# One K block and its V block held together through a pass of a four-pass attention kernel, and summed there as p k v^T

## The chip, the core and the metric

The kernel runs on one core of a Trainium2 chip. The metric is device time in microseconds (us) of one execution, compared as medians over several runs.

## The reference, cut to what matters

One decode step through attention, dense, attention, dense (each with a layer norm and a residual), and the gradients of everything with respect to the input, both caches and all weights. Both attention layers use the same caches and the same weights: 32 query heads, 4 key/value groups of 8 heads, 65,536 cached positions, head size 128, bfloat16. K and V are 64 MiB each.

```python
def _A_ref(x, k_cache, v_cache, wq, wo):
    q = (x @ wq).reshape(B, Sq, Hq, Dh).transpose(0, 2, 1, 3)
    k = jnp.repeat(k_cache, rep, axis=1)
    v = jnp.repeat(v_cache, rep, axis=1)
    scores = jnp.einsum("bhqd,bhkd->bhqk", q, k) * (Dh ** -0.5)
    p = _softmax(scores, axis=-1)
    o = jnp.einsum("bhqk,bhkd->bhqd", p, v)
    return o.transpose(0, 2, 1, 3).reshape(B, Sq, Hq * Dh) @ wo
...
x = x + _A_ref(_layernorm(x), A_k_cache, A_v_cache, A_wq, A_wo)
x = x + _B_ref(_layernorm(x), B_w1, B_b1, B_w2, B_b2)
x = x + _A_ref(_layernorm(x), A_k_cache, A_v_cache, A_wq, A_wo)
x = x + _B_ref(_layernorm(x), B_w1, B_b1, B_w2, B_b2)
...
_out, _vjp = jax.vjp(_f, A_x, A_k_cache, A_v_cache, A_wq, A_wo, ...)
```

The gradient with respect to q of one head, written for one position c with weight p_c, is dq = sum over c of p_c (v_c . dO - delta) k_c, where delta is a number for the head. It can be split: (sum p_c k_c v_c^T) dO - delta (sum p_c k_c). The two sums need K, V and p, but not dO.

## The kernel before, in words

**Four passes over the caches.** Pass 1 (`attn_fwd(0, ...)`, called at line 1643) is the forward of the first attention, pass 2 (`attn_fwd(1, ...)`, line 1683) that of the second, pass 3 (`attn_bwd3`, lines 1207 to 1295) gives dq of the second attention, pass 4 (`attn_bwd4`, lines 1298 to 1486) gives dq of the first and the gradients of both caches. Between the passes stand dense stages: 1 to 2, 2 to 3 and 3 to 4.

**Blocks and buffers.** A cache is cut into 4 groups of 16 blocks; a block is 32 columns of 128 positions, 1 MiB, written here as V(3,12): group 3, block 12. SBUF holds an arena of 20 buffers of one block each (line 267). Eight of them become "planes" with the exponentials of one layer and group (`plane`, line 276); a plane is held from when its group starts (`holds`, lines 1183 to 1185) until pass 4 is done with it. The other buffers carry K, V, weights and staged outputs. `Slot`, `take_one` and `take_pair` (lines 284 to 333) give a buffer, or two neighbours for a 2 MiB load, in the order in which they became free when the program is written. A load into a buffer waits on the chip until the buffer's last reader is done. All these loads are issued by one queue (SP), in order: a load whose buffer is not free holds up those behind it.

**The order of the work.** A pass goes through 8-column items, 256 of them. `pipeline` (line 847) runs one step per item: in pass 2 the transposes of K (`kT`, line 1023), two steps later the scores (`kS`, line 1037), 36 steps later P times V (`v8`, line 1121), and at the end of the step one piece of background work (`bg.step`, line 869), as small products with wq or wo. In passes 1 to 3 the order on TensorE, VectorE and ScalarE inside the pipeline is the written one (`manual_schedule`); in pass 4 a scheduler decides. `kv8` (line 351) loads a block when it is first touched, `kv_done` (line 377) frees it after its last item.

**Blocks kept between passes.** Each pass goes through the blocks in an order of its own (`ITEMS`, line 411). `plan_keep` (line 416) keeps 8 K blocks from pass 1 to pass 2, and 7 V blocks each from pass 2 to 3 and from 3 to 4: those that the next pass touches first. K kept from pass 1 and V kept from pass 3 are kept transposed, in place (`turned_to`, line 369); the next pass then needs no transposes for them. Pass 2 begins with K(3,12); pass 3 comes to block (3,12) in its last quarter group; pass 4 begins with the V blocks (3,15) down to (3,9), so V(3,12) is one of the 7 that pass 3 keeps.

**PSUM.** In passes 1 to 3 the pool has three banks for transposes (`ps_tr`), two for scores, one accumulator, one for the background and one for small things (`ps_mv`, line 100): the two tiny transposes of each softmax unit, among others.

The lines that the change touches:

```python
            if i is None:
                sl = Slot("blk_" + t, load=True)
                nc.sync.dma_start(out=sl.t.rearrange("p (j d) -> p j d", d=DH), in_=half(KVIN[t], g, hb))
```

Of the kernel before, what the change touches and what calls it, by code (L numbers as in the profile page):

```python
# [16 lines left out]
P = 128  # L17
# [3 lines left out]
def kernel(  # L21
# [57 lines left out]
    slotp = ctx.enter_context(tc.tile_pool(name="slotp", bufs=1))  # L79


    PS = {}

    def open_psum(stack, name, pass4=False):
        PS["pool"] = stack.enter_context(tc.tile_pool(name=name, bufs=1, space=PSUM))
# [12 lines left out]
        return PS["pool"].tile(shape, F32, name="ps_acc", tag="acc", bufs=1)  # L98

    def ps_mv(shape, dtype=F32):  # L100
        if PS["pass4"]:
            return ps_tr(shape, dtype)
        return PS["pool"].tile(shape, dtype, name="ps_mv", tag="mv", bufs=1)

    def ps_bg(shape):
        return PS["pool"].tile(shape, F32, name="ps_bg", tag="bg", bufs=1)
# [244 lines left out]
    def kv8(t, g, c8):  # L351
        hb, j = divmod(c8, J)
        key = (t, g, hb)
        have = KV["have"]
        if key not in have:
            i = None
            if NOW["pairs"] and hb % 2 == 0 and (t, g, hb + 1) not in have and key not in KV["halves"]:
                i = take_pair()
            if i is None:
                sl = Slot("blk_" + t, load=True)  # L360
                nc.sync.dma_start(out=sl.t.rearrange("p (j d) -> p j d", d=DH), in_=half(KVIN[t], g, hb))
                have[key] = sl
            else:
                for h in range(2):
                    have[(t, g, hb + h)] = Slot("blk_" + t, at=i + h)
                nc.sync.dma_start(out=wide(i).rearrange("p (j d) -> p j d", d=DH), in_=KVIN[t][g][hb // 2])
        return have[key].t.rearrange("p (j d) -> p j d", d=DH)[:, j:j + 8, :]

    def turned_to(t, g, c8, kb8):

        if KV["turn"] == t and (t, g, c8 // J) in KV["keep"]:
            state_key = (t, g, c8)
            KV["next"].add(state_key)
            return kb8
        return ktpool.tile([P, 8, P], BF, name="kt", tag="kt")

    def kv_done(t, g, c8):

        key = (t, g, c8 // J)
        if c8 % J == J - 8 and key not in KV["keep"]:  # L380
            KV["have"].pop(key).free()

    def order_by_unit(desc, unit):
# [25 lines left out]
    DV_LAG = TLEAD + 1  # L409
    V_LEAD = 4 * J // 8  # L410
    ITEMS = [order_by_unit(False, SU), order_by_unit(True, SU), order_by_unit(False, HB), order_by_unit(True, J)]
    V_SHIFT = lambda k: min(V_LEAD, max(0, (k - V_LEAD) // 3))
    TOUCH = [touch_order(ITEMS[0], [("k", 0), ("v", FWD_LAG)]), touch_order(ITEMS[1], [("k", 0), ("v", FWD_LAG)]),
             touch_order(ITEMS[2], [("v", 0), ("k", B3_LAG)]), touch_order(ITEMS[3], [("v", V_SHIFT), ("k", B4_LAG + V_LEAD)])]
# [6 lines left out]
    def start_pass(p):  # L421
        KV["keep"] = plan_keep(p)
        KV["turned"] = KV.get("next", set())
        KV["next"] = set()
        KV["turn"] = {0: "k", 2: "v"}.get(p)
        NOW["pairs"] = p < 3
        KV["halves"] = set(TOUCH[p][-8:] + (TOUCH[p][:18] if p else []))

    def f_cols(ap, nb):
        return ap[:, bass.ds(512 * (nb // 4) + nb % 4, P, step=4)]  # L430
# [353 lines left out]
    class Background:  # L784
# [8 lines left out]
        def step(self, i):  # L793
            while self.later and i >= self.later[0][0]:
                self.add(*self.later.popleft()[1:])
            while self.urgent:
                r = next(self.urgent[0][1], "end")
                if r == "end":
                    self.urgent.popleft()
                    continue  # L800
                if r == "wait":
                    break
                return
            while self.normal and self.done < self.total * i / self.steps:
                if next(self.normal[0], "end") == "end":
                    self.normal.popleft()
                else:
                    self.done += 1
                    return

        def add(self, gen, key=None):
            self.urgent.append((key, gen))
# [31 lines left out]
        for fn in TASKS.pop(i, ()):  # L844
            fn()

    def pipeline(items, stages, bg, end=(), holds=(), lead=None):

        def due(lag):
            at = {}  # L850
            for k, it in enumerate(items):
                at.setdefault(k + lag + LEAD if lead is None or lag >= 0 else k + ~lag + lead(k), []).append(it)
            return at
        LEAD = 0 if lead is None else lead(len(items))
        when = [due(l) for _, l in stages]
        maxlag = max(l for _, l in stages) + LEAD
        for i in range(len(items) + maxlag):
            NOW["i"] = i
            NOW["wide"] = NOW["pairs"]
            for at, k in holds:  # L860
                if i == at:
                    hold(k)
            tasks(i - 0.5)
            for n, (fn, lag) in enumerate(stages):
                for it in when[n].get(i, ()):
                    fn(*it)
                if n == 0:
                    tasks(i)
            bg.step(max(0, i - LEAD))
            NOW["wide"] = False  # L870
            NOW["step"] += 1
            for before, fn in end:
                if i == len(items) + maxlag - before:
                    fn()
        while TASKS:
            k = min(TASKS)
            NOW["i"] = int(k + 0.5)
            tasks(k)
# [128 lines left out]
    def attn_fwd(p, L, on_group, bg, end=()):  # L1007
# [113 lines left out]
        def v8(g, c8):  # L1121
# [7 lines left out]
            for i in range(8):  # L1129
# [2 lines left out]
                NOW["ps_o"] = nc.tensor.matmul(ps_o[:, 0:w, :], lhsT=vb8[:, i, :], rhs=E(p, g, c, w),  # L1132
                                               start=(c % SU == 0), stop=(c % SU == SU - 1), skip_group_check=True)
            kv_done("v", g, c8)
            if (c8 + 8) % SU == 0:
                first_at(1, lambda: unit_end(g, su, ps_o))

        def unit_sums(g, su):

# [43 lines left out]
        holds = [(k * n + 2, plane(p, g)) for k, g in enumerate(order) if k > 0]  # L1183
        if p == 0:
            holds.append((len(items) - 40, plane(1, ITEMS[1][0][0])))
        with tc.manual_schedule(engines=ORDERED):
            pipeline(items, [(kT, 0), (kS, TLEAD), (v8, FWD_LAG)], bg, end, holds)
        st.close()


# [16 lines left out]
    def attn_bwd3(p, L, on_group, bg, end=()):  # L1207
# [5 lines left out]
        state = {}  # L1213
        gfirst = {g: next(c8 for gg, c8 in items if gg == g) for g in range(G)}
        glast = {g: [c8 for gg, c8 in items if gg == g][-1] for g in range(G)}

        def vT(g, c8):
            bg.need(g)
# [12 lines left out]
        def vS(g, c8):  # L1231
# [5 lines left out]
            vt = state.pop(("vt", g, c8))  # L1237
            for i in range(8):
                s = (c8 + i) % HB
                if s == 0:  # L1240
                    state["ps_dp"] = ps_sc([P, HB, R])
                late = c8 + i - s == gfirst[g]
                w = min(8, HB - s)

                def delta(first):
                    nc.tensor.matmul(state["ps_dp"][:, :, :].rearrange("p c r -> p (c r)"), lhsT=sel2[:, :],
                                     rhs=state["ndt"][:, :, :].rearrange("o c r -> o (c r)"), start=first, stop=not first,
                                     skip_group_check=True)
                if s == 0 and not late:
                    delta(True)  # L1250
                nc.tensor.matmul(state["ps_dp"][:, s:s + w, :].rearrange("p a b -> p (a b)"), lhsT=vt[:, i, :],
                                 rhs=dOpad[:, g, 0:w, :].rearrange("p a b -> p (a b)"), start=late and s == 0,
                                 stop=(s == HB - 1) and not late, skip_group_check=True)
                if s == HB - 1 and late:
                    delta(False)
            if is_turned("v", g, c8):
                kv_done("v", g, c8)
            if (c8 + 8) % HB == 0:
                c0 = c8 + 8 - HB
                ps_dp = state["ps_dp"]  # L1260

                def ds():
# [6 lines left out]
        def k8(g, c8):  # L1269
            kb8 = kv8("k", g, c8)  # L1270
            dsT = state[("ds", g, c8 // HB)]
            if c8 % SU == 0:
                state["ps_dq"] = ps_acc([P, 8, R])
            ps_dq = state["ps_dq"]
            for i in range(8):
                c = c8 + i
                s = c % HB
                w = min(8, HB - s)
                nc.tensor.matmul(ps_dq[:, 0:w, :].rearrange("p a b -> p (a b)"), lhsT=kb8[:, i, :],
                                 rhs=dsT[:, s:s + w, :].rearrange("p a b -> p (a b)"),  # L1280
                                 start=(c % SU == 0), stop=(c % SU == SU - 1), skip_group_check=True)
            kv_done("k", g, c8)
            if (c8 + 8) % SU == 0:
                su = c8 // SU

                def fold():
                    fold_dq(L, g, su, ps_dq[:, 0, :], gfirst[g] // SU == su, glast[g] // SU == su, dspool)
                    if glast[g] // SU == su:
                        on_group(g)
                first_at(1, fold)  # L1290
# [294 lines left out]

    def open_dense(name):
        st = ExitStack()
        DENSE["pool"] = st.enter_context(tc.tile_pool(name=name, bufs=1))
        return st

# [89 lines left out]
    def on2(g):  # L1680
        if g != lastg[1]:
            bg.add(g_wo(L3, x3, g))
    attn_fwd(1, L3, on2, bg, [(3, pre_load("wo3", lambda: wo_slabs(lastg[1], 2)))])
    bg.drain()

# [29 lines left out]
    def ch_turn(s, js=range(4), to=None):  # L1715

        n = ch_pe(s)
        for j in js:
            pt = ps_tr()
            for kc in range(n):  # L1720
                nc.tensor.transpose(pt[:, kc, :], ch_cols(s, kc, j), ident_b[:, :])
            wt = DENSE["pool"].tile([P, 8, P], BF, name="wt", tag="wt", bufs=8)
            (nc.vector.tensor_copy if (to[j] if to else j == 3) else nc.scalar.copy)(out=wt[:, 0:n, :], in_=pt[:, 0:n, :])
            w1t[(s, j)] = wt

# [132 lines left out]
            bg.add(g_dn(L3, dn3, g, g == firstg[2]))  # L1858
    attn_bwd3(2, L3, on3, bg, [(10, pre_load("wq3", lambda: wq_slabs(lastg[2], 2)))])
    bg.drain()  # L1860


    reset_load()
# [202 lines left out]
```

## Time and profile before

| what | value |
|---|---|
| three runs, us | 1934.89, 1932.82, 1929.56 (median 1932.82) |
| the profiled execution, its own time | 1938.19 us |
| its span, first to last instruction | 1936.3 us |
| mean granted TensorE clock | 0.918 |
| busy: TensorE, VectorE, ScalarE, GpSimd | 82%, 61%, 54%, 7% |
| moved by DMA | 787.62 MB, mean 407 GB/s |

By stage, from the profile's stretches (DMA share is the mean busy share of the 16 DMA engines; it can come out a little above 1):

| stretch, us | stage | TensorE busy | DMA share | GB/s |
|---|---|---|---|---|
| 0 to 365 | pass 1 | 282.31 | 1.00 | 419 |
| 365 to 415 | dense 1 to 2 | 37.69 | 1.01 | 413 |
| 415 to 741 | pass 2 | 263.17 | 1.00 | 419 |
| 741 to 781 | dense 2 to 3 | 37.43 | 0.94 | 320 |
| 781 to 1117 | pass 3 | 271.89 | 1.00 | 418 |
| 1117 to 1172 | dense 3 to 4 | 46.14 | 0.86 | 322 |
| 1172 to 1900 | pass 4 | 622.96 | 1.00 | 408 |
| 1900 to 1936 | last outputs | 22.12 | 0.64 | 262 |

How to read it: a stage with a DMA share of 1 goes as fast as its bytes come; where the share falls, something else ends last. In the timeline rows below, a row is the start, the duration, the engine, the line and the operation; "SPq" is the queue that issues the loads, and a gap between its rows is time in which the next load waited for its buffer.

### The profile page before, as it was taken

The numbers are of one execution on the slowest core, as the hardware profiler recorded it, in microseconds if no ns is written. First come the engines' busy times: TensorE is split into PE (matmuls) and PEld (weight loads), VectorE is DVE, ScalarE is ACT, GpSimd is POOL, SyncE is SP. The second block draws the span as 40 slices with busy tenths as digits, with TensorE's granted clock in tenths as the row PEclk, the third lists the DMA queues.
The fourth block names the chain that finished last, engine by engine and source line by source line (L and its number), as shares of the span: only waits on it lengthen the run. The fifth ranks groups of instructions, "written<-read, shape, count | busy, mean of one in ns | idle before, by whom it ended". The sixth has DMA issues, their size and how long they took to land. (4 is left out here: it accounts for less than half of the span.)

```text
span 1936.3 us, 66770 instructions
## 1 busy us (share of the span) xinstructions
PE 1583.7 (82%) x30099; PEld 1294.0 (67%) x30099; DVE 1172.8 (61%) x2447; ACT 1045.2 (54%) x1620; POOL 143.6 (7%) x325
## 2 busy tenths in 40 slices
PE   6878778588778878978787888778889889688896
PEld 6878777578778878877677776445555556455563
DVE  5645555255555654545454577767867678667685
ACT  3434334245343545436363465757867677567675
POOL 0000000000000000000000002111211111111111
PEclk9989999789998999999999998988988889888896
DMA  9999999999999999999999997999999999999997
GB/s 394 427 427 424 428 429 415 404 421 395 429 425 427 427 419 335 395 426 428 426 420 425 405 363 283 425 422 381 424 424 423 420 399 407 409 415 396 405 421 301
DMA packets 107148, 787.62 MB, mean 407 GB/s; under 512 B 9440, under 2 KB 16622, under 8 KB 42222
## 3 DMA queue, kind: packets, MB, share of 16 engines
q1 hardware_dynamic: 78558, 609.26, 76.2%
q0 software_dynamic: 24080, 165.70, 20.6%
q10 hardware_dynamic: 4224, 8.39, 1.1%
q8 instruction: 235, 3.85, 0.7%
q14 instruction: 51, 0.42, 0.1%
HBM read 617.62 MB, written 165.69 MB: 405 GB/s over the span
## 5 line engine op out<-in xcount | busy, mean ns | idle before, releaser
L164 DVE COPY kt<-ps_tr 128x1024 bf16<-128x1024 bf16 (+1 forms) x733 | 503.3, 688 | 435.7 <-PE ps_tr L1031 237.9
L161 ACT CAST arena<-ps_gg 128x1024 bf16<-128x1024 f32 x457 | 444.4, 1012 | 201.9 <-PE ps_gg L1435 132.0
L1031 PE MATMUL ps_tr<-ident_b,arena 128*128 128x128 bf16 x3840 | 309.1, 225 | 49.3 <-DMA arena<-in_A_k_cache_dram 35.6
L161 ACT COPY kt<-ps_tr 128x1024 bf16<-128x1024 bf16 (+1 forms) x179 | 187.4, 1053 | 185.8 <-PE ps_tr L1225 103.1
L164 DVE CAST arena<-ps_gg 128x1024 bf16<-128x1024 f32 (+2 forms) x186 | 222.3, 1195 | 82.4 <-PE ps_gg L1435 44.4
L1031 PEld LDWEIGHTS <-arena 128*128 128x128 bf16 x3840 | 232.6, 101 | 58.4 <-DMA arena<-in_A_k_cache_dram 38.1
L1132 PE MATMUL ps_acc<-arena 128*128 128x64 bf16 (+4 forms) x4096 | 203.1, 195 | 50.5 <-DMA arena<-in_A_v_cache_dram 32.4
L1435 PE MATMUL ps_gg<-GG,xt 64*128 64x512 bf16 x1024 | 214.3, 414 | 22.0 <-ACT arena L161 10.6
L1354 PE MATMUL ps_tr<-ident_b,arena 128*128 128x128 bf16 x1824 | 179.5, 234 | 38.1 <-DVE kt L164 18.6
L1049 PE MATMUL ps_sc<-L_qpad,kt 128*128 128x64 bf16 (+7 forms) x3584 | 183.1, 194 | 20.8 <-issue 11.0
L1114 ACT ACTIVATE arena<-S_sb,L_negm 128x128 bf16<-128x128 f32 x256 | 165.2, 1006 | 59.4 <-DVE L_negm L1099 51.9
L1132 PEld LDWEIGHTS <-arena 128*128 128x128 bf16 x4096 | 158.2, 100 | 56.6 <-DMA arena<-in_A_v_cache_dram 36.6
L1225 PE MATMUL ps_tr<-ident_b,arena 128*128 128x128 bf16 x2000 | 159.3, 224 | 43.9 <-DMA arena<-in_A_v_cache_dram 42.0
L1354 PEld LDWEIGHTS <-arena 128*128 128x128 bf16 x1824 | 118.9, 104 | 94.2 <-issue 72.8
L1049 PEld LDWEIGHTS <-kt 128*128 128x128 bf16 x3584 | 152.3, 100 | 25.1 <-issue 12.2
L1225 PEld LDWEIGHTS <-arena 128*128 128x128 bf16 x2000 | 120.6, 100 | 49.5 <-DMA arena<-in_A_v_cache_dram 44.7
L1466 PEld LDWEIGHTS <-arena 128*128 128x128 bf16 x2048 | 90.8, 101 | 59.8 <-issue 29.9
L1114 ACT ACTIVATION_READ_ACCUMULATOR arena<-S_sb,L_negm 128x1 f32 x256 | 128.2, 501 | 0.0
L1391 PE MATMUL ps_sc<-DOB,kt 128*128 128x64 bf16 (+3 forms) x1824 | 117.6, 197 | 0.1
L1391 PEld LDWEIGHTS <-kt 128*128 128x128 bf16 x1824 | 84.6, 101 | 48.7 <-issue 47.2
L585 ACT ACTIVATE mv_t<-mv_t 128x1024 bf16<-128x1024 bf16 x96 | 102.0, 1064 | 24.2 <-DVE mv_t L596 24.1
L1466 PE MATMUL ps_acc<-X,arena 128*128 128x64 bf16 (+3 forms) x1536 | 94.7, 197 | 23.5 <-DMA arena<-in_A_k_cache_dram 23.5
(320 smaller groups left out, 2106.0 us busy)
## 6 DMA issues: line engine op xcount, KB each, us to landing
arena<-in_A_k_cache_dram SPq DMA_DIRECT2D x82, 2048.0 KB, 20.7
arena<-in_A_v_cache_dram SPq DMA_DIRECT2D x79, 2048.0 KB, 21.0
out_dram<-arena POOLq DMA_DIRECT2D x149, 1024.0 KB, 15.6
arena<-in_A_v_cache_dram SPq DMA_DIRECT2D x84, 1024.0 KB, 12.5
arena<-in_A_k_cache_dram SPq DMA_DIRECT2D x84, 1024.0 KB, 12.9
arena<-in_A_wo_dram SPq DMA_DIRECT2D x22, 1024.0 KB, 14.9
arena<-in_B_w_dram SPq DMA_DIRECT2D x21, 1024.0 KB, 10.4
arena<-in_A_wq_dram SPq DMA_DIRECT2D x7, 2048.0 KB, 26.2
```

The source lines that it names most:

```text
L161: nc.scalar.copy(out=out, in_=in_)
L164: nc.vector.tensor_copy(out=out, in_=in_)
L585: nc.scalar.activation(out=t[:, :], in_=t[:, :], func=ACTF.Copy, accum_out=y[:, kc:kc + 1])
L1031: nc.tensor.transpose(pt[:, i, :], kb8[:, i, :], ident_b[:, :])
L1049: nc.tensor.matmul(state["ps_s"][:, s:s + w, :].rearrange("p a b -> p (a b)"), lhsT=kt[:, i, :], rhs=L["qpad"][:, g, 0:w, :].rearrange("p ...
L1114: nc.scalar.activation(out=E(p, g, c0, SU)[:, :, h], in_=S[:, h, :], func=ACTF.Exp, bias=L["negm"][:, g, su, h:h + 1], scale=SCALE, accum_ ...
L1132: NOW["ps_o"] = nc.tensor.matmul(ps_o[:, 0:w, :], lhsT=vb8[:, i, :], rhs=E(p, g, c, w), start=(c % SU == 0), stop=(c % SU == SU - 1), skip ...
L1225: nc.tensor.transpose(pt[:, i, :], vb8[:, i, :], ident_b[:, :])
L1354: nc.tensor.transpose(pt[:, i, :], vb8[:, i, :], ident_b[:, :])
L1391: nc.tensor.matmul(state["ps_dp"][:, s:s + w, :].rearrange("p a b -> p (a b)"), lhsT=vt[:, i, :], rhs=DOB[:, g, 0:w, :].rearrange("p a b - ...
L1435: nc.tensor.matmul(pg[:, 512 * h:512 * h + 512], lhsT=xt[64 * h:64 * h + 64, j1 // 8 + m, :], rhs=gg[64 * h:64 * h + 64, :, :].rearrange(" ...
L1466: nc.tensor.matmul(ps_dq[:, 0:w, :].rearrange("p a b -> p (a b)"), lhsT=kb8[:, i, :], rhs=X[:, s:s + w, :].rearrange("p a b -> p (a b)"), ...
```

## The change

Block (3,12), the first that pass 2 touches, is taken out of pass 3 (`ITEMS[2]`). For it pass 2 sums p k v^T for each of the 8 heads of the group (`PKV["m"]`, 128 x 8 x 128, fp32) and p k (`PKV["s"]`), and pass 3 turns these into the block's part of dq by a few small products (`pkv_dq`), added where the unit's dq is folded.

- K(3,12) is still kept from pass 1, but no longer transposed in place: pass 2 transposes it.
- V(3,12) goes into the buffer beside K(3,12) (`i ^ 1`), which is that of K(3,13), and both stay until the sums are made.
- `g_pkv` is a side job of pass 2: one piece per step in which the background did nothing. A piece multiplies 128 x 128 of K by p of four heads on GpSimd (a 128 x 512 product, 64 in all) and multiplies V by an earlier one on TensorE into a PSUM bank, two pieces behind. Four times it adds eight small products for p k.
- That bank is the one of `ps_mv`, so in pass 2 the small things take `ps_tr` banks.
- The dense stage 2 to 3 takes half of its `wt` buffers from the `kt` pool, to make room for `PKV`.
- The plan of what pass 3 keeps for pass 4 (`plan_keep`) is untouched.

```diff
     def ps_mv(shape, dtype=F32):
-        if PS["pass4"]:
+        if PS["pass4"] or PS["m"]:
             return ps_tr(shape, dtype)
...
+    def ps_m():
+        return PS["pool"].tile([P, 4, P], F32, name="ps_m", tag="mv", bufs=1)
...
             if i is None:
-                sl = Slot("blk_" + t, load=True)
+                at = None
+                if key in KV["long"]:
+                    at = have[("k", MG, MB)].i ^ 1
+                    del FREE[at]
+                sl = Slot("blk_" + t, at=at, load=True)
...
-        if KV["turn"] == t and (t, g, c8 // J) in KV["keep"]:
+        if KV["turn"] == t and (t, g, c8 // J) in KV["keep"] and (t, g, c8 // J) != MKEYS[0]:
...
-        if c8 % J == J - 8 and key not in KV["keep"]:
+        if c8 % J == J - 8 and key not in KV["keep"] and key not in KV["long"]:
             KV["have"].pop(key).free()
...
+    MG, MB = ITEMS[1][0][0], ITEMS[1][0][1] // J
+    ITEMS[2] = [(g, c8) for g, c8 in ITEMS[2] if (g, c8 // J) != (MG, MB)]
+    MKEYS = [(t, MG, MB) for t in "kv"]
...
-            bg.step(max(0, i - LEAD))
+            if not bg.step(max(0, i - LEAD)) and sides:
+                if next(sides[0], "end") == "end":
+                    sides.popleft()
...
+        def g_pkv(g, hb):
+            ks, vs = (KV["have"][(t, g, hb)] for t in "kv")
+            k3, v3 = (sl.t.rearrange("p (j d) -> p j d", d=DH) for sl in (ks, vs))
+            nc.vector.memset(PKV["s"][:], 0.0)
+            for hf in range(2):
+                acc = ps_m()
+                made = deque()
+                def product():
+                    j, r = made.popleft()
+                    nc.tensor.matmul(acc[:, :, :].rearrange("p a b -> p (a b)"), lhsT=v3[:, j, :],
+                                     rhs=r[:, :, :].rearrange("p a b -> p (a b)"), start=j == 0, stop=j == J - 1)
+                for j in range(J):
+                    r = spool.tile([P, 4, P], BF, name="pk", tag="pk", bufs=3)
+                    e4 = E(p, g, hb * J + j, 1)[:, 0, 4 * hf:4 * hf + 4]
+                    nc.gpsimd.tensor_tensor(out=r[:, :, :], in0=k3[:, j, :].unsqueeze(1).to_broadcast([P, 4, P]),
+                                            in1=e4.unsqueeze(2).to_broadcast([P, 4, P]), op=ALU.mult)
+                    made.append((j, r))
+                    if len(made) > 2:
+                        product()
+                    if hf == 0 and j % 8 == 4:
+                        pk = ps_tr([P, R], F32)
+                        for i in range(8):
+                            jj = j - 4 + i
+                            nc.tensor.matmul(pk[:, :], lhsT=k3[:, jj, :], rhs=E(p, g, hb * J + jj, 1)[:, 0, :], start=i == 0, stop=i == 7)
+                        nc.vector.tensor_tensor(out=PKV["s"][:], in0=PKV["s"][:], in1=pk[:, :], op=ALU.add)
+                    yield
+                while made:
+                    product()
+                yield
+                nc.scalar.copy(out=PKV["m"][:, 4 * hf:4 * hf + 4, :], in_=acc[:, :, :])
+            for key in MKEYS:
+                KV["have"].pop(key).free()
...
+        def pkv_dq():
+            pt = ps_mv([P, 2, R])
+            for h in range(R):
+                nc.tensor.matmul(pt[:, 0, h:h + 1], lhsT=PKV["m"][:, h, :], rhs=L["dOT"][:, MG * R + h:MG * R + h + 1], start=True, stop=True)
+            nc.tensor.matmul(pt[:, 1, :], lhsT=sel2[:, :], rhs=L["nd2"][:, gsl(MG)], start=True, stop=True)
...
-            wt = DENSE["pool"].tile([P, 8, P], BF, name="wt", tag="wt", bufs=8)
+            DENSE["n"] += 1
+            if DENSE["n"] % 2:
+                wt = ktpool.tile([P, 8, P], BF, name="kt", tag="kt")
+            else:
+                wt = DENSE["pool"].tile([P, 8, P], BF, name="wt", tag="wt", bufs=4)
```

The rest of the diff makes pass 3 find the first and last item of a unit and of a group in a list with a gap, and adds `pkv_dq`'s result in `fold`.

## The prediction

> **What bounds the kernel now.** I read the page's 40 slices first, then stretches by stage, then the queue that issues the loads. The slices of the page:
>
> ```profile
> DMA  9999999999999999999999997999999999999997
> GB/s 394 427 427 424 428 429 415 404 421 395 429 425 427 427 419 335 395 426 428 426 420 425 405 363 283 425 422 381 424 424 423 420 399 407 409 415 396 405 421 301
> ```
>
> The transfers fill every slice but one and the last, at some 425 GB/s where only K and V move. So a byte less is time less, 1 MiB (1.0486 MB) being 2.47 us at 424 GB/s, provided that the DMA engines are not made to wait elsewhere. Where do they wait now? The stretches say it (stretch, its length, then busy us of TensorE, its weight loads, VectorE, ScalarE, GpSimd, then granted clock, DMA share, GB/s):
>
> ```profile
> 435.00:445.00 10.00, 9.30 (x241) 8.96 (x240) 5.75 (x11) 6.97 (x20) 0.00 (x0) 1.00 0.74 286
> 450.00:550.00 100.00, 82.13 (x1995) 78.60 (x1993) 57.00 (x132) 44.96 (x109) 0.00 (x0) 0.97 1.01 426
> 650.00:735.00 85.00, 66.04 (x1617) 62.79 (x1615) 42.95 (x108) 40.30 (x104) 0.00 (x0) 0.96 1.00 421
> 900.00:1050.00 150.00, 116.13 (x2604) 108.33 (x2605) 73.06 (x150) 68.08 (x93) 0.00 (x0) 0.93 1.01 424
> 1117.00:1165.00 48.00, 39.85 (x896) 37.56 (x896) 38.86 (x95) 35.08 (x42) 1.84 (x14) 1.00 0.97 366
> 1165.00:1195.00 30.00, 26.96 (x436) 18.82 (x437) 17.76 (x49) 14.84 (x17) 5.16 (x11) 0.83 0.61 229
> ```
>
> Passes 2 and 3 run at a DMA share of 1, with TensorE busy 78 to 82% and GpSimd not at all. There are two holes that matter here: 2.6 us (26% of 10) early in pass 2, and 11.7 us (39% of 30) where pass 4 starts.
>
> **Pass 3: two blocks less.** K(3,12) and V(3,12) are not loaded: 2 x 2.47 = **-4.9 us**, since the share is 1 there and TensorE waits for data. If TensorE were the bound in the last quarter it would be about half, -2.5, since four items less go through it at most once a microsecond; and -5.2 at the 406 GB/s of the pass's last 67 us. The nine small products of `pkv_dq` (a pair of fp32 products took 0.34 us at line 212, so 1.5 us at most) hide under that waiting; the four missing items free more.
>
> **But V(3,12) comes back in pass 4.** It is one of the 7 V blocks that pass 3 used to leave in SBUF, and the plan is untouched. The built program's list of loads shows it: 581.09 MiB issued by SP before, 580.09 after, one block less and not two. The new load stands early in pass 4, ahead of K(3,13), in a buffer that falls free with the last weight product of the dense stage (1167.7 us). Its 2.47 us fit into the 11.7 us hole: 0, or +2.5 if the loads behind it are late by it. Pass 4 must also transpose it: 32 transposes, 8 in 0.45 us in the rows below, make 1.8 us in a stretch where TensorE is busy 27 of 30 us; I take **+1.5**, between 0 and +4 (with a wait for the block itself). Four copies of 0.7 to 1.0 us lie in VectorE's idle 12 us. The buffer that pass 3 no longer keeps lets the dense stage load one block further ahead; its share of 0.97 leaves 1.4 us to gain, and I take half, **-0.7**.
>
> **Pass 2, the start: a load that blocks the queue.** V(3,12) must go into the buffer of K(3,13). The queue's timeline:
>
> ```profile
> 401.87 0.34 SPq L361 DMA_DIRECT2D arena<-in_A_k_cache_dram  x1
> 404.69 0.34 SPq L361 DMA_DIRECT2D arena<-in_A_v_cache_dram  x1
> 407.01 0.33 SPq L361 DMA_DIRECT2D arena<-in_A_k_cache_dram  x1
> 411.24 0.33 SPq L361 DMA_DIRECT2D arena<-in_A_v_cache_dram  x1
> 412.24 0.38 SPq L459 DMA_DIRECT2D arena<-in_A_wq_dram  x1
> 413.87 0.33 SPq L361 DMA_DIRECT2D arena<-in_A_k_cache_dram  x1
> 417.49 0.33 SPq L361 DMA_DIRECT2D arena<-in_A_v_cache_dram  x1
> ...
> 426.61 0.33 SPq L366 DMA_DIRECT2D arena<-in_A_v_cache_dram  x1
> 439.94 0.33 SPq L366 DMA_DIRECT2D arena<-in_A_k_cache_dram  x1
> ```
>
> The row at 404.69 is V(3,12), into a buffer of the dense stage. The row at 417.49 is the one that got K(3,13)'s buffer, when its scores were done. In the changed program V(3,12) waits for that, at about 418, as three of the block's four transposes stand ahead of the pass's first scores and the last one's copy adds about 0.5 us. Queued behind it are K(3,6), V(3,13), half a wq and K(3,7), whose buffers are long free. Nothing is issued from 402 to 418. A block took 12.3 us (median) to land here, so the engines run dry at 414.4 and start again about 1 us after the issue: 5 us idle. In return, 11 MiB are then issued in some 9 us, enough to 446, so that the old hole at 435 to 445 closes. Net 5 - 2.6 = **+2.4**; at least 0 (the issue comes as early as 415), at most +6 (idle 6, hole kept).
>
> **Pass 2, the stretch of the sums.** A step moves half a MiB, 1.23 us at 426 GB/s. Where data is there, TensorE does it in 0.92 us:
>
> ```profile
> 438.38 0.61 PE L1031 MATMUL ps_tr<-ident_b,arena 128*128 128x128 bf16 x8
> 438.83 0.40 PE L1049 MATMUL ps_sc<-L_qpad,kt 128*128 128x64 bf16 x8
> 439.06 0.40 PE L1132 MATMUL ps_acc<-arena 128*128 128x64 bf16 x8
> 439.30 0.61 PE L1031 MATMUL ps_tr<-ident_b,arena 128*128 128x128 bf16 x8
> ```
>
> The product with 512 columns adds about 0.21 (the 512-column row of line 1386 took 0.37, a one-column product 0.16, the difference being columns): 1.13 of 1.23 us, before the clock (0.91 to 0.97 in this stretch) takes its part: 1.2. It just fits. The 32 products for p k (8 of one column in 0.34 us) and the 32 transposes add some 3 us over the stretch. What hides all this is the queue: a 2 MiB load takes 20.7 us (median) to land, so four are under way. One pair is now held, leaving six; the old program goes through the pass's last two groups with six pairs, at 421 GB/s (the row 650 to 735). So TensorE may fall back some 10 us before a DMA engine stands still. I take **+1**, between 0 and +10. The banks that `ps_mv` now shares are asked for twice a unit of 16 steps, and two banks a round cover a copy of 0.7 us; nothing. The `wt` change keeps eight buffers in turn; nothing.
>
> **GpSimd's product** is not in the trace; its nearest rows:
>
> ```profile
> L1363 POOL COPY xin<-arena 128x512 bf16<-128x512 bf16 x64 | 39.8, 622 | 123.9 <-PE ps_tr L1369 102.6 <-PE ps_mv L205 21.0
> L1334 POOL CAST CC<-cf 128x128 bf16<-128x128 f32 x32 | 11.8, 383 | 40.3 <-PE ps_tr L1336 32.6 <-DVE cf L1329 5.1 <-issue 2.5
> ```
>
> It cannot be quicker than the copy of that size, 0.62 us. Two operands as two copies are 1.24 us; at the cast's pace, which spreads a narrow operand as here (383 less the 95 of the shortest memset, over 128: 2.25 ns an element), one operand is 1.25 and two 2.4. I take 1.25: one step. Up to about 1.4 it costs nothing, since 64 x 0.16 us are the 10 us of the queue. TensorE waits for it in order, and K's transposes stand behind that wait.
>
> The Trainium skill (GPSIMD Engine Reference, section 3.1) gives some 2.6 cycles an element at 1.2 GHz for two inputs, and advises VectorE for such work. That would be an estimated 1.1 us for 512 elements; no run here shows it yet, and by it the sum stays as it is.
>
> **The sum**: -4.9 + 0 + 1.5 - 0.7 + 2.4 + 1 = **-0.7 us**. Against the profiled execution's 1938.19 (span 1936.3 and 1.9 around it) that is 1937.5; it ran 5.4 above the median of the runs, 1932.82, to which I apply the same: **1932**. A measurement of this kernel tells 0.3% (5.8 us) from no change; this is within. The bounds together give -6.6 (-5.2 - 1.4) to +20 (-2.5 + 2.5 + 4 + 6 + 10).
>
> **Rivals.**
> - *GpSimd sets the pace, slower.* Every step with a product then lasts as long as one on GpSimd. It decides from 1.4 us on; at 1.8, midway between 1.25 and 2.4, it costs 64 x 0.57 - 10 = 26 us: 1959. For it: the cast's slope. Against: two copies are 1.24.
> - *The queue runs short, slower.* With one pair fewer and TensorE almost full, holes like the one at 435 come back. Three of 2.6 us, none of the first closed (+2.6), give 10.4 more than forecast: 1942. For it: that hole arose with all pairs in use. Against: the rate with six pairs late in the pass.
> - *Both blocks pay and the rest is hidden, faster.* The blocked queue costs nothing net, and the dense stage gains its 1.4: 1932.8 - 6.6 = 1926. For it: the shares of 1. Against: the 16 us without an issue.
>
> **Chances.** Forecast 0.50, all of it within 0.3%. GpSimd's pace 0.16 and the short queue 0.14, both slower by over 0.3%; all hidden 0.20, faster by over 0.3%. So faster 0.20, same 0.50, slower 0.30. Range 1924 to 1950: it takes in the fast rival, the short queue and the milder half of GpSimd's.
>
> **What would show it.** A gap in the queue from about 402 to 418 and a DMA share near 0 at 414 to 419, with none at 435 to 445. GpSimd's product at about 1.25 us, and TensorE not waiting for it; share 1 up to 560. Pass 3 shorter by 5 us. V(3,12) loaded about 1168 us plus what pass 2 and 3 moved, landing before its transposes. I am wrong if the share falls during the sums, or if pass 3 gets shorter by much less than two blocks.

## The result, and the profile after

The changed kernel takes **1952.64 us** (median of 6 runs, 1949.96 to 1962.77); the kernel before, run beside it, 1932.55 (6 runs). The ratio is **1.0108, 95% interval 1.0081 to 1.0135**: some 21 us slower. The forecast was 1932, range 1924 to 1950. The profiled execution took 1953.13 us (span 1951.3), near its median; that of before (1938.19) was one of its slower ones, so the two profiles lie only 15.0 us apart. For sizes the ratios count, for places the profiles.

The two rows of the page's slices, after:

```profile
DMA  9999999989999999999999988899999999999997
GB/s 394 426 427 425 428 428 416 399 342 425 428 426 428 428 416 335 392 409 429 424 425 422 404 346 322 339 359 392 421 424 422 410 425 394 424 422 423 423 405 298
```

Two places are new: one slice near 400 us (342 GB/s, 421 before), and the stretch from about 1170 to 1365 us (322, 339, 359, 392; before 283, 425, 422, 381), of which the second and the third slice are clearly lower. The stretches say how much (stretch, length, busy us of TensorE, weight loads, VectorE, ScalarE, GpSimd, granted clock, DMA share, GB/s). After:

```profile
435.00:445.00 10.00, 9.95 (x250) 9.18 (x247) 5.66 (x11) 6.49 (x19) 4.08 (x4) 1.00 1.03 433
450.00:550.00 100.00, 86.68 (x1950) 78.41 (x1946) 58.81 (x129) 40.30 (x98) 48.83 (x47) 0.97 1.01 426
650.00:735.00 85.00, 66.45 (x1577) 63.17 (x1573) 45.86 (x109) 36.50 (x88) 0.00 (x0) 0.95 1.00 421
900.00:1050.00 150.00, 120.32 (x2667) 111.88 (x2665) 75.87 (x156) 70.22 (x97) 0.00 (x0) 0.91 1.01 425
1117.00:1165.00 48.00, 41.36 (x956) 38.90 (x954) 38.40 (x89) 34.56 (x42) 1.16 (x13) 1.00 0.92 357
1165.00:1195.00 30.00, 25.96 (x511) 19.77 (x509) 19.78 (x61) 13.64 (x16) 5.38 (x11) 1.00 0.75 284
1195.00:1320.00 125.00, 96.24 (x1033) 56.44 (x1032) 77.23 (x138) 72.36 (x84) 19.39 (x38) 0.76 0.89 346
```

and the last of these stretches before, which the prediction did not look at:

```profile
1195.00:1320.00 125.00, 102.20 (x1279) 64.62 (x1279) 89.95 (x164) 82.04 (x97) 22.98 (x43) 0.88 0.99 409
```

The hole at 435 is not there (what that is worth is said further down), and the stretch of the sums has a share of 1.01 with GpSimd at work. The loss is in the last row: 125 us in which the share falls from 0.99 to 0.89 and every engine does less.

To place it, four events were read in each trace: the last product with V of pass 2, the first and last transposes of pass 3, and the first and last products with K of pass 4. Us from the span's start:

| kernel | last V, pass 2 | pass 3, first | pass 3, last | pass 4, first K | pass 4, last K |
|---|---|---|---|---|---|
| before | 740.7 | 781.0 | 1105.1 | 1174.9 | 1901.7 |
| after | 748.3 | 787.6 | 1108.7 | 1175.0 | 1917.8 |

Pass 2 loses 7.6 us; pass 3 and the dense stages give it back; pass 4 takes 742.8 us, not 726.8. **In these two profiles the whole loss lies in pass 4**, in whose function the change edits no line. It is complete early: the last product with K of pass 4's first cache group comes at 1358.9 us, before at 1340.4.

In the changed kernel's timelines of ScalarE (first fence; idle time before a row, and what ended it, in brackets) and of TensorE (second):

```profile
1191.21 1.01 ACT L164 CAST arena<-ps_gg 128x1024 bf16<-128x1024 f32 x1 [0.48 <-PE ps_gg L1517]
1205.64 1.93 ACT L164 CAST arena<-ps_gg 128x1024 bf16<-128x1024 f32 x2 [13.42 <-DMA out_dram<-arena]
```

```profile
1206.70 0.61 PE L1595 MATMUL ps_gg<-rowb,rowa 2*128 2x512 bf16 x2 [7.11 <-ACT arena L164]
```

ScalarE stands 13.4 us because it may not write into a buffer whose output is still on its way to HBM, and TensorE 7.1 us behind it. Buffers that this work frees come free later for the loads.

**The theory** (A). The staging ring is the set of buffers in which outputs may be staged. In pass 4 the end of a kept V block does three things: it frees a buffer, makes the next of four loads that are listed ahead (`nexts`), and, with the fourth, opens the staging ring, so that buffers freed later join it. V(3,12) was the kept block whose end made the fourth load, V(3,7). It is no longer kept, so the fourth load waits for block (3,11), 5 steps later in the program. There it takes the buffer of the first dV output; the ring opens late, and the first dK output goes into the buffer of the second dV output, one step after that output is issued; in the kernel before, the buffer of the first dK output had been issued five steps earlier. These are facts of the two programs; that they cost the time is the theory. In the queue's timeline V(3,7) moves from 1180.08 us (first fence, before) to 1192.32 us (second, the first of the two V loads), behind a wo load that it preceded:

```profile
1180.08 0.33 SPq L361 DMA_DIRECT2D arena<-in_A_v_cache_dram  x1
```

```profile
1184.65 0.33 SPq L470 DMA_DIRECT2D arena<-in_A_wo_dram  x1
1190.65 0.33 SPq L368 DMA_DIRECT2D arena<-in_A_k_cache_dram  x1
1192.32 2.64 SPq L368 DMA_DIRECT2D arena<-in_A_v_cache_dram  x2
```

**The rivals**: (B) the sums, the blocked queue and the held pair; (C) the load and the turning of V(3,12) themselves.

### The profile page after: what moved, and what is told of

Its sections match the earlier page's. It is cut to its first block, busy times and chain, and to the rows that moved or that the text cites. A ratio compares the mean times of both kernels' runs of the same rounds, so it can differ in the third digit from the quotient of the medians.

```text
span 1951.3 us, 67030 instructions
## 1 busy us (share of the span) xinstructions
PE 1608.7 (82%) x30180; PEld 1307.7 (67%) x30180; DVE 1178.0 (60%) x2460; ACT 1048.5 (54%) x1621; POOL 208.7 (11%) x389
## 5 line engine op out<-in xcount | busy, mean ns | idle before, releaser
L167 DVE COPY kt<-ps_tr 128x1024 bf16<-128x1024 bf16 x741 | 508.6, 688 | 441.7 <-PE ps_tr L1045 240.9
L164 ACT CAST arena<-ps_gg 128x1024 bf16<-128x1024 f32 (+1 forms) x460 | 447.4, 1013 | 220.4 <-PE ps_gg L1517 158.9
L164 ACT COPY kt<-ps_tr 128x1024 bf16<-128x1024 bf16 x183 | 191.1, 1047 | 210.4 <-PE ps_tr L1298 109.5
L1045 PEld LDWEIGHTS <-arena 128*128 128x128 bf16 x3872 | 238.3, 101 | 56.0 <-DMA arena<-in_A_k_cache_dram 35.6
L1063 PE MATMUL ps_sc<-L_qpad,kt 128*128 128x64 bf16 (+3 forms) x3648 | 186.8, 194 | 24.5 <-issue 15.3
L1146 PEld LDWEIGHTS <-arena 128*128 128x128 bf16 x4096 | 159.4, 101 | 50.5 <-DMA arena<-in_A_v_cache_dram 32.4
L1063 PEld LDWEIGHTS <-kt 128*128 128x128 bf16 x3648 | 155.2, 100 | 30.1 <-issue 18.7
L1436 PEld LDWEIGHTS <-arena 128*128 128x128 bf16 x1856 | 121.7, 104 | 71.5 <-issue 58.6
L1548 PEld LDWEIGHTS <-arena 128*128 128x128 bf16 x2048 | 92.5, 103 | 95.9 <-DMA arena<-in_A_k_cache_dram 60.8
L1298 PEld LDWEIGHTS <-arena 128*128 128x128 bf16 x1968 | 119.6, 101 | 42.9 <-DMA arena<-in_A_v_cache_dram 39.8
L1473 PEld LDWEIGHTS <-kt 128*128 128x128 bf16 x1856 | 87.1, 102 | 48.4 <-issue 46.6
L1473 PE MATMUL ps_sc<-DOB,kt 128*128 128x64 bf16 (+1 forms) x1856 | 119.1, 198 | 0.3 <-ACT kt L164 0.3
L1523 POOL DMA_DIRECT2D out_dram<-arena x128 | 68.3, 534 | 432.5 <-ACT arena L164 243.9
## 6 DMA issues: line engine op xcount, KB each, us to landing
arena<-in_A_v_cache_dram SPq DMA_DIRECT2D x78, 2048.0 KB, 20.9
out_dram<-arena POOLq DMA_DIRECT2D x149, 1024.0 KB, 17.2
```

The lines of the kernel that those rows point to most:

```text
L164: nc.scalar.copy(out=out, in_=in_)
L167: nc.vector.tensor_copy(out=out, in_=in_)
L1045: nc.tensor.transpose(pt[:, i, :], kb8[:, i, :], ident_b[:, :])
L1063: nc.tensor.matmul(state["ps_s"][:, s:s + w, :].rearrange("p a b -> p (a b)"), lhsT=kt[:, i, :], rhs=L["qpad"][:, g, 0:w, :].rearrange("p ...
L1298: nc.tensor.transpose(pt[:, i, :], vb8[:, i, :], ident_b[:, :])
L1436: nc.tensor.transpose(pt[:, i, :], vb8[:, i, :], ident_b[:, :])
```

## The experiments

Each ratio is to the kernel before, run on the same chip; "us" is the ratio less one, times 1933.

| kernel | ratio | 95% interval | us |
|---|---|---|---|
| after | 1.0108 | 1.0081 to 1.0135 | +20.9 |
| e1, before, V(3,12) not kept | 1.0080 | 1.0064 to 1.0097 | +15.5 |
| e2, after, fourth load at its old place | 1.0047 | 1.0030 to 1.0065 | +9.1 |
| e3, after, V in any buffer | 1.0088 | 1.0069 to 1.0107 | +17.0 |
| e4, after, block (3,8) | 1.0021 | 1.0001 to 1.0041 | +4.1 |
| e5, after, V(3,12) loaded, not turned | 1.0017 | 0.9999 to 1.0034 | +3.3 |
| e6, before, V(3,12) turned twice | 1.0035 | 1.0017 to 1.0052 | +6.8 |
| e7, after, no sums | 1.0089 | 1.0070 to 1.0108 | +17.2 |
| e8, as e4, V in any buffer | 1.0006 | 0.9991 to 1.0022 | +1.2 |
| e9, before, 8 V blocks kept | 1.0149 | 1.0130 to 1.0168 | +28.8 |
| e10, as e4, no sums | 1.0004 | 0.9992 to 1.0015 | +0.8 |
| e11, after, ring opened earlier | 1.0071 | 1.0056 to 1.0086 | +13.7 |
| e12, before, four blocks turned twice | 1.0040 | 1.0019 to 1.0060 | +7.7 |
| e13, as e12, no copies | 1.0028 | 1.0008 to 1.0048 | +5.4 |

**e1: the lost block alone, in the kernel before**

```diff
-return set([... if k[0] == "kvv"[p]][:NKEEP[p]])
+return set([... if k[0] == "kvv"[p]][:NKEEP[p]]) - ({("v", 3, 12)} if p == 2 else set())
```

> The kernel before, with one thing of the change alone: pass 3 no longer keeps its turned block of V(3,12) for pass 4, which loads and turns it again. No sums, nothing skipped in pass 3, no block held in pass 2. Theory A (the loss lies in pass 4: without the kept block the fourth of the next loads is made a block later, takes a staging buffer, and the staging ring runs into an output that is still being written): about +12 to +17 us on the kernel before, and holes in the transfers between 1195 and 1320 us like those of the changed kernel (shares of 0.81 to 0.96 where before has 1.01). Theory B (the loss comes from the sums, the queue block in pass 2 and the pair held): 0 to +2.5 us, for 32 transposes and one load, and no holes there.

Measured +15.5 us, with the stretch of the changed kernel:

```profile
1195.00:1320.00 125.00, 93.76 (x1011) 55.78 (x1009) 79.38 (x143) 77.00 (x90) 20.38 (x39) 0.78 0.89 347
```

The same share and all but the same GB/s, without a sum, and ScalarE's longest wait for an output is 13.1 us here too. Three quarters of the loss come with this one block; rival B is not the main cause.

**e2: the fourth load back at the end of block 12**

```diff
 kv_done("v", g, c8)                  # vT, a block that is not kept
+if c8 % J == J - 8 and nexts:
+    NOW["newest"] = True
+    kv8(*nexts.popleft())
+    NOW["newest"] = False
+    NOW["ring"] = not nexts
```

> The changed kernel, with the fourth of pass 4's next loads made again at the end of block 12, as the kernel before makes it; V(3,12) is still loaded and turned again. Theory A (order of the loads and the staging buffers): -12 to -15 us on the changed kernel, so about 1938 to 1941 us, with shares near 1.01 from 1195 to 1300 us. Theory C (the extra load and its transposes are themselves what costs in pass 4, for the transfers are what bounds it): no more than -3 us on the changed kernel. Theory B (sums and pass 2): no change.

```profile
1195.00:1320.00 125.00, 101.23 (x1135) 60.87 (x1134) 83.24 (x151) 77.79 (x92) 20.80 (x40) 0.80 0.94 367
```

+9.1 us, so about 12 of the 21 us go (9.6 by the medians); at 1195 to 1240 us the share is back at 1, and ScalarE's longest wait for an output is 3.2 us. It is at the lower edge of what A expected, or below it. From 1240 to 1320 us the share is still 0.87 to 0.96, which makes 7.2 us idle where before has 2.2: something else costs time there.

**e11: the ring alone** (the fourth load stays late)

```diff
-NOW["newest"] = True
+NOW["newest"] = len(nexts) > 1
...
-NOW["ring"] = not nexts
+NOW["ring"] = len(nexts) < 2
```

> The changed kernel, in which the staging ring of pass 4 opens one fetch earlier, so that two more buffers join it; the fourth next load stays where the change has put it, at the end of block 11, and still goes into the buffer of the first dV output. Theory A1 (what costs is the wait for an output that is still being written: ScalarE 13.4 us, TensorE 7.1 us): these two waits go, -7 to -12 us on the changed kernel. Theory A2 (what costs is that V(3,7) is fetched a block later): the waits go, the time stays, 0 to -3 us on the changed kernel.

ScalarE's waits for outputs from 1165 to 1360 us (total us, times, longest), after and then e11:

```profile
ACT arena L164 <- DMA out_dram<-arena: 16.1, 3, 13.4
```

```profile
ACT arena L164 <- DMA out_dram<-arena: 7.2, 2, 3.8
```

Before has 19.5 us of them in ten waits, the longest 3.9: small ones belong to a stretch in which transfers are the bound. The long wait is gone in e11, and +20.9 became +13.7: about 7 us, at the edge of A1 (4.3 by the medians). VectorE got one such wait instead, 7.7 us. The two intervals (1.0056 to 1.0086, 1.0081 to 1.0135) just overlap. So the output wait is part of what the order costs, about half of it by these figures; that the late load is the rest is only the difference, and no run shows it by itself.

**e5: the load without the turning**

```diff
+if p == 3:
+    KV["turned"] = KV["turned"] | set(("v", MG, MB * J + c) for c in range(0, J, 8))
```

> The changed kernel, in which pass 4 loads V(3,12) again but takes it as it is, without the 32 transposes and their four copies (its share of the output is then not the product that is wanted); the block is freed and the fourth next load is made where the kernel before does it. What is left of the change in pass 4 is the load alone. The run with the order of the loads mended (1943 us) still lost some 10 us from the first K product of pass 4 to the end of its first stretch (1340 us before, 1350 there). Theory T (the turning holds the TensorE, which is busy 82 to 84% there, and its copies): that loss is gone, the stretch ends near 1341 to 1343 us, total 0 to +3 us on the kernel before. Theory L (the load and the buffer that it takes from the loads behind it): the stretch still ends near 1348 to 1351 us, total +7 to +10 us.

```profile
1195.00:1320.00 125.00, 106.89 (x1298) 67.10 (x1297) 91.48 (x168) 82.29 (x97) 24.01 (x45) 0.85 0.98 403
```

+3.3 us, and the last K product of the first group comes at 1343.5 us (1340.4 before, 1350.4 in e2). This kernel loads V(3,12) again, and its pass 4, from first to last K product, takes 724.0 us (726.8 before). So **the load costs nothing that can be measured**, and what comes with the turning is what e2 still paid: 1.0047 against 1.0017, two intervals that overlap a little.

**e6, e12, e13: the turning without a load, in the kernel before**

```diff
 if is_turned("v", g, c8):
     state[("vt", g, c8)] = vb8
+    if (g, c8 // J) == (3, 12):          # e12, e13: c8 // J in (9, 10, 11, 12)
+        pt = ps_tr()
+        for i in range(8):
+            nc.tensor.transpose(pt[:, i, :], vb8[:, i, :], ident_b[:, :])
+        vt = ktpool.tile([P, 8, P], BF, name="kt", tag="kt")      # this and the rest not in e13
+        evac(vt[:, :, :], pt[:, :, :])
+        state[("vt", g, c8)] = vt
```

> The kernel before, in which pass 4 turns its kept block V(3,12) once more (the block is then the wrong way round, so this block's share is not the product that is wanted): 32 transposes and four copies more, no load more, no buffer less, the same order. Theory T: +7 to +10 us on the kernel before, first stretch of pass 4 ending near 1348 to 1350 us. Theory L: 0 to +2 us.

> The kernel before, in which pass 4 turns four of its seven kept V blocks, (3,9) to (3,12), once more: 128 transposes and 16 copies, no load, no buffer, no order changed (these blocks are then the wrong way round, so their share is not the product that is wanted). One block cost +6.8 us. If every block turned in the first stretch costs as much: +20 to +28 us on the kernel before. If it was only the place of (3,12), the last block before the loads run on: +6 to +10 us.

> The same 128 transposes without their 16 copies; the kept blocks are used as they are, so that the right product is computed. Theory P (TensorE is the bound in the first stretch): at least three quarters of what the run with the copies costs. Theory C (the copies on VectorE and ScalarE, both over 95% busy in parts of the stretch, or waiting for them): a quarter of it at most.

One block +6.8 (a little under what T expected; the last K product of the first group comes at 1345.1 us), four blocks +7.7, four without copies +5.4 us. The three intervals overlap: the cost is there with one block, does not grow as the blocks do, and most of it seems to stay without the copies (5.4 of 7.7, just under the three quarters that P asked for). So neither the copies nor an equal price per block explains it; theory P is the nearer one. At 1165 to 1195 us the share is 0.61 before, 0.55 in e6, 0.48 in e12 and 0.54 in e13, which is 1.8 to 3.9 us more of idle transfers: part of the cost lies there. What moves is the load queue. Its timeline before, and then in e13:

```profile
1193.80 0.33 SPq L459 DMA_DIRECT2D arena<-in_A_wo_dram  x1
1197.10 0.33 SPq L361 DMA_DIRECT2D arena<-in_A_v_cache_dram  x1
```

```profile
1202.38 0.33 SPq L459 DMA_DIRECT2D arena<-in_A_wo_dram  x1
1208.05 0.33 SPq L361 DMA_DIRECT2D arena<-in_A_v_cache_dram  x1
```

The load of wo waits for the buffer of the last kept V block. TensorE is busy 27 of 30 us at 1165 to 1195, so transposes put ahead of that block's products should free the buffer later: the load is 8.6 us later in e13, 4.0 in e12. In e6 this load is not late (1192.42), but the second half of wo is (1211.89 against 1203.06). Why the cost does not grow with the number of blocks stays open; pass 4's order is a scheduler's and shifts with each edit.

**e9: one more block kept, not one less**

```diff
-NKEEP = [8, 7, 7]
+NKEEP = [8, 7, 8]
```

> The kernel before, with one more V block (8, not 7) kept and turned by pass 3 for pass 4. Theory T (a block turned in the first stretch of pass 4 costs some 6 us there, as the last runs have it): the reverse is won, about -6 us in pass 4 for V(3,8), whose load of 2.5 us goes too; against it the dense stage has a buffer less to load ahead with, which cost the run that kept one block less about 3.5 us the other way. Net -2 to -5 us on the kernel before. Theory R (the staging ring and the buffers decide, not the turning): one buffer less where pass 4 begins, +5 to +15 us.

+28.8 us: theory T is refuted as a rule for savings. R had the direction, but not the size: it expected +5 to +15. This kernel saves a load and a turning. Its waits of ScalarE at 1165 to 1360 us, and its stretch:

```profile
ACT arena L161 <- DMA out_dram<-arena: 31.1, 9, 9.9
```

```profile
1195.00:1320.00 125.00, 102.82 (x1061) 59.88 (x1059) 77.91 (x135) 72.36 (x85) 18.28 (x36) 0.69 0.87 343
```

Nine waits, the longest 9.9 us, where before has ten of at most 3.9. One kept block less, or one more, changes the hand-out of buffers where pass 4 begins, and each costs far more than a block's transfer. That the waits make the whole of e9's loss was not tried.

**e3 and e7: what pass 2 pays**

```diff
-at = have[("k", MG, MB)].i ^ 1                                           # e3
+at = min((t, i) for i, t in FREE.items() if i < NSLOT)[1]
```

e7 replaces the body of `g_pkv`: two memsets, the same number of yields, the same free at the end.

> The changed kernel, with V(3,12) of pass 1 and 2 put into the oldest free buffer instead of K(3,12)'s neighbour. The order of issue has then no load that waits for a buffer at 402 to 418 us, but two pairs of buffers are broken up instead of one. If the 17 us in which SP issues nothing are what pass 2 loses: checkpoints of pass 2 come about 5 us earlier (the last V row of pass 2 near 743 us, not 748), total -3 to -6 us if pass 4 keeps its loss. If it is the missing pair that makes pass 2 late: the same or later, 0 to +10 us.

> The changed kernel without the sums: no GpSimd products, no products of 512 columns, no p k, no copies of their banks; p k v^T and p k are zeros (so dq of this block is left out). The pair of buffers is held as long as before and both blocks are skipped in pass 3. Theory S (the sums' work slows pass 2, whose last V row comes 7.6 us later than before): -3 to -6 us on the changed kernel, the last V row of pass 2 near 743 to 745 us. Theory H (the stop of the queue at 402 to 418 us and the pair that is held): no change, last V row at 747 to 749 us.

In e3 the queue does not stop (share 1.04 and 1.01 at 400 to 420 us). The last V row of pass 2 comes at 743.8 us in e3 and at 744.0 in e7, against 747.8 in the mean of the four kernels with both costs (after, e2, e5, e11: 746.3 to 748.8) and 739.6 in the mean of the six that have neither (before, e1, e6, e9, e12, e13: 739.0 to 740.7). So pass 2 loses 8.1 us, **about 4 by the blocked queue and about 4 by the sums**. In the total both runs come out 4 us lower, as expected, though the intervals overlap. That the missing pair alone makes pass 2 late (the second case of e3, and H of e7) is ruled out by these rows.

**e4, e8, e10: the block (3,8)**, which pass 3 did not keep for pass 4 anyway. Both loads are then saved for good (579.09 MiB issued by SP, 581.09 before), and pass 4 has its old order.

```diff
-MG, MB = ITEMS[1][0][0], ITEMS[1][0][1] // J
+MG, MB = ITEMS[1][16][0], ITEMS[1][16][1] // J
...
-del FREE[at]
+HELD.discard(at)         # and HELD.add(KV["have"][MKEYS[0]].i ^ 1) where pass 2 starts; e8: as e3
```

> The changed kernel, with the block (3,8) taken in place of (3,12); the neighbour of K(3,8)'s buffer is held free for V(3,8). V(3,8) is none of the blocks that pass 3 keeps for pass 4, so both of its loads in pass 3 are saved for good and the order of pass 4 is as before; V(3,8) is loaded later in pass 2. Theory A: no holes from 1195 to 1320 us, no stop of SP at 402 to 418 us, and the 4.9 us that pass 3 was to save remain, less up to 3 us for the sums: 1927 to 1933 us, so -5 to 0 on the kernel before. Theory B (sums and a pair held cost by themselves): +5 us or more on the kernel before, most of it visible at the end of pass 2.

> The changed kernel with block (3,8), and with V(3,8) in the oldest free buffer instead of the neighbour of K(3,8)'s, which is then not held from the start of pass 2. With the neighbour held this block lost 4.9 us up to the last V row of pass 2 (745.6 us), 2.6 of it by a hole of the transfers at 435 to 445 us that was twice that of the kernel before. If the held buffer made that hole: the hole goes back to about 2.6 us, last V row near 743 us, total 2 to 3 us below the run with the neighbour held: 1933 to 1935 us. If a second broken pair costs as much again: no gain, or up to 3 us slower than that run.

> The changed kernel with block (3,8), its neighbour held as in the first run of that block, and without the sums (zeros in their place, so dq of this block is left out). It shows what the change is worth at most, if the sums cost nothing. Theory S (the sums cost 3 to 4 us of pass 2, as the run without them on block (3,12) has it): 3 to 4 us below the run with the sums, so 1 to 4 us below the kernel before. Theory H (the pair that is held costs what pass 2 loses): as the run with the sums, 0 to +4 us on the kernel before.

+4.1, +1.2 and +0.8 us. Pass 4 is as before again: from its first to its last K product 724.8 us in e4 (726.8 before), and

```profile
1195.00:1320.00 125.00, 104.64 (x1285) 65.53 (x1281) 90.35 (x165) 82.41 (x98) 23.13 (x44) 0.85 0.99 409
```

With V(3,12) kept, pass 4's loss is gone; but e4 missed the forecast of theory A (0 to -5), and none of the three beats the kernel before. In e4 pass 2 ends at 745.6 us. In e10, without any sums, it ends at 742.8, still 3.2 us later than in those six kernels, and pass 3 is 3.8 us shorter (321.8 against 325.6): what holding the block saves in pass 3 is nearly lost in pass 2. There is a hole at 435 to 445 us of 4.8 us in e10 (share 0.52; 0.48 in e4). e8 was expected to close it; it grew (share 0.26), though this was the slowest of e8's twelve executions (1945.41, median 1936.68), and e8's total is no worse than e4's.

One caution on that hole. The six kernels are the same program up to the end of pass 2, and their shares at 435 to 445 us are 0.74 (before), 0.77, 0.79, 0.88, 0.99 and 1.00. So the same program has a hole of 0 to 2.6 us there, 1.4 in the mean, and the 2.6 of before was one execution's. The five kernels whose queue is blocked (after, e2, e5, e7, e11) have none (shares 1.01 to 1.03), so the change does close it, but it closes 1.4 us in the mean. The holes of e4, e8 and e10 are larger than any of the six.

## Why the prediction was wrong, step by step

**The step that failed**: "But V(3,12) comes back in pass 4", costed as a load (0) and 32 transposes (+1.5, at most +4). Pass 4 got 16.0 us longer. The load is 0, as forecast (e5). With the transposes come about 6 us, not 1.5 (e2 against e5; e6), and why stays open: four blocks of them cost hardly more than one (e12). The largest part, about 12 us (after against e2; these parts go by the ratios, the 16.0 by two executions), was not in the sum: I priced the operations added and not **what the kept block sets off**. I wrote that the load takes a buffer from the dense stage, and did not ask whose fetch that buffer had served, nor which buffer the first outputs would get. The list of loads with their buffers, which I used to count MiB, already had V(3,7) in a staged output's buffer, after a wo load that it had preceded. e1, which changes only that V(3,12) is not kept, loses 15.5 us.

**Pass 2, the start: +2.4.** Right in place, small in size:

```profile
402.13 0.34 SPq L368 DMA_DIRECT2D arena<-in_A_k_cache_dram  x1
418.80 0.34 SPq L368 DMA_DIRECT2D arena<-in_A_v_cache_dram  x1
```

No load is issued in between, as forecast. But the engines do not run dry all at once at 414.4: the share is 0.81 at 400 to 415 and 0.11 at 415 to 420, which makes 7.6 us idle with the 0.3 after that. Less the hole of 2.6 it is 5.0, less the mean hole of 1.4 it is 6.2; the rows of e3 say about 4. The credit of 2.6 for the hole rested on one execution.

**The stretch of the sums: +1.** About 4 (e7's row), inside 0 to +10, and not by a hole: the share is 1.01 throughout. TensorE is busy 86.7 us of 100 where it was 82.1; that it therefore comes later to the end of the pass is my reading, and no run separates it. I looked for the cost only in the transfers.

**GpSimd's product.** Line 1170 and the product that waits for it, line 1165 (ns: min, median, max; then first and last start):

```profile
L1170 POOL TENSOR_TENSOR pk<-arena x64: 1035/1040/1042, 428.0 to 563.0; 128x512 bf16<-128x512 bf16 x64
L1165 PE MATMUL ps_m<-pk,arena x64: 376/380/615, 439.8 to 565.0; 128*128 128x512 bf16 x64
...
  PE ps_m L1165: 0.2, 1
```

1.04 us, I took 1.25. It is under a step, and TensorE waited for it 0.2 us in all (last row). The rival in which GpSimd sets the pace is out. The estimate worked out from the Trainium skill's figure (GPSIMD Engine Reference, section 3.1) was 1.1 us; this trace agrees with it.

**Pass 3: -4.9.** Measured -4.65: 320.95 us in the mean of after, e2, e5 and e11, 325.6 in the mean of the six kernels that skip nothing. The two profiles alone give -3.0.

**The dense stage: -0.7.** From the last transposes of pass 3 to the first K product of pass 4 it is 69.15 us in the mean of before, e4, e8 and e10, and 65.83 in the mean of the six with a block less kept and turned in pass 4 (after, e1, e2, e3, e7, e11): -3.3. The end of this interval depends on pass 4's order too.

Up to pass 4 the errors nearly cancel: forecast -2.2 us, measured +0.1 between the two profiles. That near agreement is luck in part: the dense stage gained more and pass 2 lost more than forecast. Without the order and the turning (e5) the kernel is +3.3 (-0.2 to +6.6), which can't be told from no change.

**The other rivals.** No queue ran short: the rows at 450 and 650 have shares of 1.01 and 1.00. Nor was all hidden: pass 2 lost 8.1 us. None of the cases of the prediction contained pass 4's buffers.

## What to carry to other kernels

When a change takes a buffer or a kept block out of a plan, price what its release sets off (the next fetch, the opening of a ring, the next output's buffer) before the operations; compare the two programs' lists of buffers, not only their bytes. Look for the loss also where a stage begins with full buffers and a full TensorE, even if the change edits no line of it. Before a hole of the transfers is counted as a gain, see whether it is there in a second execution. A transfer saved where another buffer must be held to save it can be paid back: here three versions that saved 2 MiB for good were no faster.

## What the runs showed of the hardware that was not expected

GpSimd's product of two spread operands, 128x512 in bfloat16, took 1.04 us, less than two copies of that size (2 x 0.62). When the load queue stopped here (402.13 to 418.80 us), the DMA engines did not fall idle at one moment: the share was 0.81 over 400 to 415 us and then 0.11. And over 1195 to 1320 us, where TensorE stood and started again, the granted clock was lower: 0.76 after and 0.69 in e9, 0.88 before; which is cause and which effect was not tried. A lower clock is not needed for a loss: e13 has 0.90 there and loses 5.4 us.
